# A fifth written order for stage one, with more of its loads held behind TensorE steps

## The chip, the cores and the metric

The kernel runs on one core of one Trainium2 chip. Its time is device microseconds of one execution, and a figure for a kernel is the median of several runs. The profile is one more execution, whose own time stands beside its span below.

## The reference

Three blocks follow one another; all is float32. The change is in the first.

```python
# block 1: per (batch 4, head 8), S = 576, D = 64
q_d, k_d, v_d = means over 4 neighbouring rows           # S/4 = 144 rows
out_up = repeat(softmax(scale * q_d @ k_d.T) @ v_d, 4)
mask = abs(i - j) < 4                                    # a local window
out = out_up + softmax(where(mask, scale * q @ k.T, -1e9)) @ v
# block 2: h = gelu(x @ w_in); u, v = halves; v normalised over features
x = x + (u * (w_sg @ v + b_sg)) @ w_out
# block 3: 4 experts of causal attention, top-2 gate by x @ w_gate
```

## The kernel before

The 4 x 8 heads go in 16 units u of two heads each (4 batches x 4 pairs); the functions below belong to `phase1`, the stage that takes about the first quarter of the span. One unit is these steps, named by a short name and the unit's number:

- Loads, all on SyncE's queue (SP): `lq`, `lk` (288 KB each), `lv` (288 KB, for the pooled branch), `lw` (320 KB, the windows of v). Their buffers come in rings, so that `lq`u and `lk`u also wait for unit u-3's transposes, `lv`u for `V`u-2, `lw`u for `Do`u-3.
- TensorE (PE): `Aq`, `Ak` transpose q and k; `Bm`, `Bs` write the mask and the windowed scores; `Bd` the pooled scores; `Cc`, `Ca` transpose the two softmax results; `Du`, `Do` multiply them with v.
- ScalarE (ACT): copies out of PSUM `aq`, `ak`, `cb`, `ca`, `du`, the exponentials `ey` and `ex`, small ones `yb`, `ne`.
- VectorE (DVE): `akd` (pooled k), maxima `ym`, `xm`, `xs` (subtract), sums `sx`, reciprocal `n`, and `dx`, which adds the two branches into `xT`.
- GpSimd (POOL): `aqd` (pooled q), `V` (pooled v), and the normalising multiplies `ny`, `nx`.

Woven in between is work for block 2: eight pieces of w_in are loaded (`fetch0` to `fetch7`, 512 KB each) and split into a high and a low part by `size` (ACT), `clamp`, `bits`, `stt1`, `stt2` (DVE), `hi` and `lo` (POOL). When all of batch 0 is in `xT`, `xhi` and `xlo` split it, and `mul0` to `mul3` (PE) are block 2's first products, with `gelu` behind each. `small` loads g_ln and b_sg. After stage one block 2 goes on with transposes of w_sg (`pwsg`, its loads `wsg` come next on SP) and the tiles `dv`, which read what `lo4` to `lo7` wrote.

Nothing of this is scheduled at run time. `ORDER` is a list of all 609 steps; the program is written out in that order, so each engine, and SP, does its own steps in the order in which the list has them, and a step that waits holds every later one of its engine. `GATE` names loads that additionally wait until a PE step has run: `lw0:Bm3` means that `lw0` is issued after `Bm3`. Behind a held load on SP every later load waits too.

PSUM has three `wide` tiles (two banks each: `Aq`, `Ak`, `Bm` with `Bs`, `Cc`, `Ca`, `Do`, `mul`) and two `narrow` ones (`Bd`, `Du`, `size`). `Steps.run` gives a step the tile that comes free first by its own table of costs, the first in its sequence where several are equal; a tile comes free when its readers are done.

Of the kernel before, what the change touches and what calls it, by code (L numbers as in the profile page):

```python
# [8 lines left out]
F32 = mybir.dt.float32  # L9
# [7 lines left out]
P = 128  # L17
# [3 lines left out]
def raw(ap):  # L21
# [1 line left out]


ORDER = """
    lk0 Ak0 lq0 lq1 lk1 Aq0 ak0 lq2 lk2 Aq1 aq0 Ak1 Bm0 aqd0 akd0 ak1 Bd0 aq1 Bs0 Aq2 aqd1 aq2 lq3 aqd2 Ak2
    akd1 ym0 xm0 Aq3 yb0 ak2 lq4 lk3 xs0 lv0 ey0 Bm1 Bd1 akd2 Bs1 ym1 xm1 aq3 V0 xs1 Ak3 ex0 ak3 sx0 Aq4 Bm2
    lk4 lk5 yb1 lq5 Bd2 ne0 aqd3 akd3 ey1 Bs2 n0 lv1 ny0 ex1 nx0 ym2 aq4 xm2 Ak4 xs2 ak4 sx1 aqd4 lk6 ex2 Bd3
    Bm3 akd4 Cc0 Ca0 lv2 sx2 ne1 yb2 Bs3 cb0 ym3 n1 nx1 fetch0 lq6 Ak5 ca0 ey2 Aq5 ak5 lq7 aq5 xm3 Ca1 yb3 xs3
    lw0 ny1 Cc1 Bm4 ne2 V1 ey3 Bd4 n2 akd5 ym4 ny2 Bs4 lk7 Du0 xm4 ca1 ex3 xs4 Ak6 cb1 du0 nx2 sx3 ak6 lv3 ex4  # L30
    Du1 yb4 du1 Cc2 lw1 aqd5 Do0 Bm5 fetch2 ne3 akd6 sx4 cb2 Bd5 dx0 ym5 fetch1 ey4 ne4 Bs5 size0 V2 Ca2 Aq6
    ca2 n3 yb5 aq6 ny3 lw2 V3 lw3 ey5 n4 xm5 Aq7 Ak7 clamp0 ak7 Du2 xs5 aq7 aqd6 bits0 nx3 stt10 Do1 stt20 Bm6
    Bd6 du2 dx1 Cc3 ex5 sx5 cb3 Ca3 ny4 ne5 ym6 hi0 ca3 Bs6 aqd7 lk8 yb6 Cc4 akd7 cb4 Do2 xm6 nx4 n5 Bd7 lq8
    xs6 lv4 Bm7 Ca4 nx5 ey6 dx2 ex6 ca4 ym7 Bs7 Du3 lk9 lo0 sx6 lv5 xm7 lq9 Aq8 ny5 ne6 lq10 Ak8 du3 V4 n6 yb7
    size1 xs7 Do3 clamp1 aq8 ey7 lw4 Ca5 nx6 Du4 lk10 ex7 ak8 ca5 V5 aqd8 du4 Cc5 fetch3 bits1 dx3 stt11 size2
    Ca6 akd8 lq11 Ak9 clamp2 bits2 cb5 stt21 Aq9 stt12 ak9 ny6 Do4 sx7 aq9 ca6 Bd8 aqd9 dx4 Bm8 Cc6 ym8 ne7 Bs8
    yb8 stt22 Ak10 Du5 cb6 xm8 ey8 n7 lv7 hi1 Aq10 ak10 xs8 akd9 Bm9 du5 lo1 akd10 size3 Bd9 clamp3 lv6 ny7
    aq10 Bs9 ym9 nx7 ex8 xm9 aqd10 yb9 lw5 fetch4 lk12 Aq11 Cc7 ey9 bits3 lk11 Bd10 lq12 lw6 xs9 Bm10 aq11
    stt13 V6 Do5 aqd11 ym10 lv8 Bs10 cb7 Ca7 yb10 ey10 stt23 ex9 Du6 dx5 sx8 V7 xm10 hi2 Ak12 du6 ca7 sx9 Du7
    lq13 ne8 Ak11 ak12 Aq12 size4 n8 xs10 ny8 ak11 lo2 aq12 clamp4 Bm11 akd12 nx8 Do6 V8 akd11 ne9 du7 aqd12  # L40
    Cc8 n9 Bd11 lk13 Bs11 dx6 lw7 ym11 bits4 fetch5 ex10 lq14 cb8 Ca8 stt14 xm11 yb11 sx10 Aq13 lk14 ey11 nx9
    lw8 Du8 xs11 ca8 aq13 ny9 Ak13 Do7 hi3 aqd13 ne10 stt24 ex11 dx7 n10 sx11 Bm12 Bd12 ak13 du8 Cc9 size5 Ca9
    ym12 ny10 nx10 lv9 akd13 Bs12 cb9 clamp5 Cc10 xm12 ca9 ne11 Ak14 n11 cb10 yb12 ak14 lo3 bits5 xs12 Aq14 Do8
    Bm13 hi4 ey12 lk15 lq15 ny11 V9 stt15 Bd13 aq14 ex12 dx8 Bs13 Ak15 aqd14 lv10 ym13 Aq15 stt25 nx11 ak15
    yb13 sx12 aq15 akd15 akd14 Du9 lw9 ne12 V10 Ca10 du9 xm13 Cc11 n12 xhi0 Bd14 ca10 xs13 nx12 lv11 xhi2 xlo2
    Do9 dx9 cb11 ym14 ey13 xhi1 Bm14 Ca11 ny12 Bs14 ca11 Du10 xm14 xs14 lw10 lv12 yb14 aqd15 Cc12 V11 hi5 Ca12
    du10 lw11 xhi3 fetch7 Bd15 V12 lo5 cb12 ey14 Bm15 xlo3 xlo1 Do10 xlo0 Bs15 Du11 ex13 lv13 ca12 sx13 ne13
    dx10 ym15 du11 lo4 ex14 size7 yb15 lw12 xm15 mul1 xs15 ey15 mul2 clamp7 ex15 fetch6 gelu1 sx14 Du12 bits7
    ne14 n13 gelu2 stt17 n14 V13 small ny13 du12 Do11 Do12 sx15 lw13 stt27 nx14 hi7 ne15 nx13 mul0 ny14 n15
    dx12 Cc13 dx11 size6 gelu0 Cc14 cb13 Ca14 clamp6 lo7 Ca13 Du13 ca14 cb14 lv14 ny15 ca13 lw15 lv15 lw14 Cc15  # L50
    bits6 nx15 stt16 mul3 cb15 V14 stt26 du13 Ca15 Do13 ca15 dx13 V15 Du14 gelu3 hi6 Du15 du15 lo6 Do14 Do15
    du14 dx14 dx15
""".split()
# [96 lines left out]
def tile_pooled_local_attention_gmlp_moe_attention(  # L150
# [50 lines left out]
    px = {}  # L201
# [52 lines left out]
    def phase1():  # L254
        with tc.tile_pool(name="s1", bufs=2, reuse_waits="tile") as p:
# [7 lines left out]
            pw = px["p"].tile([P, 2, 512], F32, name="wide", bufs=1)  # L263
# [260 lines left out]
            def d_x(u):  # L524
# [907 lines left out]
    with psum("ps1") as px["p"]:  # L1432
        phase1()
# [39 lines left out]
```

## Time and profile before

| what | us |
|---|---|
| median of 3 runs | 523.68 (521.07 to 525.8) |
| the profiled execution, its own time | 520.51 |
| span of that execution, first to last instruction | 518.5 |

The profiled execution has 2.0 us around its span, and lies 3.2 us under the median of the runs. Times below count from the start of the span. Stage one on PE goes from its first transpose at 5.63 us to the first `pwsg` transpose of block 2.

### The profile page before, as it was taken

The numbers are of one execution on the slowest core, as the hardware profiler recorded it, in microseconds if no ns is written. First come the engines' busy times: TensorE is split into PE (matmuls) and PEld (weight loads), VectorE is DVE, ScalarE is ACT, GpSimd is POOL, SyncE is SP. The second block draws the span as 40 slices with busy tenths as digits, with TensorE's granted clock in tenths as the row PEclk, the third lists the DMA queues.
The fourth block names the chain that finished last, engine by engine and source line by source line (L and its number), as shares of the span: only waits on it lengthen the run. The fifth ranks groups of instructions, "written<-read, shape, count | busy, mean of one in ns | idle before, by whom it ended". The sixth has DMA issues, their size and how long they took to land.

```text
span 518.5 us, 13684 instructions
## 1 busy us (share of the span) xinstructions
PE 504.5 (97%) x5405; PEld 460.9 (89%) x5405; DVE 350.3 (68%) x914; ACT 268.1 (52%) x676; POOL 252.9 (49%) x390
## 2 busy tenths in 40 slices
PE   9998898999999999999999999999999999999996
PEld 6986786889889899989998999999988989998885
DVE  4887898895869764542344137468699678868862
ACT  2886685785454450234013403356668558556761
POOL 4789689799253620360035106736447234333530
PEclk9999998999999999999999999999999999999999
DMA  8999599486500220000000001200000100011013
GB/s 204 224 226 191 153 212 210 109 202 164 163 1 2 82 61 1 1 0 1 1 1 0 1 1 31 73 2 2 2 0 1 43 21 22 21 42 43 20 62 102
DMA packets 43415, 35.02 MB, mean 68 GB/s; under 512 B 29976, under 2 KB 36376, under 8 KB 43352
## 3 DMA queue, kind: packets, MB, share of 16 engines
q1 hardware_dynamic: 43352, 34.15, 27.4%
q8 instruction: 43, 0.70, 0.6%
q14 instruction: 20, 0.16, 0.1%
HBM read 29.42 MB, written 4.72 MB: 66 GB/s over the span
## 4 chain that ended last, share of the span: by engine, by line
PE 83%; DVE 9%; issue 3%; ACT 2%; POOL 1%; DMA 1%; SPq 0%; ACTq 0%; DVEq 0%; POOLq 0%
PE wide L84 17%; PE f L84 10%; PE e L84 9%; PE du L84 7%; PE dv L84 6%; PE v L84 5%; PE i L84 5%; PE sc L84 5%; PE av L84 4%; PE gq L84 4%; PE gk L84 4%; PE tr L84 4%; PE narrow L84 3%; DVE xhla L606 1%; DVE wmn L694 1%
## 5 line engine op out<-in xcount | busy, mean ns | idle before, releaser
L249 POOL TENSOR_TENSOR gT<-z,gT 128x576 fp32r<-128x576 f32 x15 | 23.0, 1536 | 105.3 <-ACT gT L221 105.3
L1204 POOL TENSOR_SCALAR xT<-xT,sden,wt 128x128 f32<-128x128 f32 (+1 forms) x64 | 38.9, 609 | 57.8 <-DVE sden L1202 41.4
L84 PE MATMUL e<-wsgT,vn 128*128 128x288 f32 x384 | 56.6, 296 | 0.0
L84 PEld LDWEIGHTS e<-wsgT,vn 128*128 128x128 f32 x384 | 53.0, 188 | 0.3 <-DVE wsgT L735 0.2
L84 PE MATMUL f<-gT,wouts 128*128 128x288 f32 x384 | 52.1, 296 | 0.0
L84 PEld LDWEIGHTS f<-gT,wouts 128*128 128x128 f32 x384 | 51.4, 188 | 0.2 <-DVE wouts L701 0.2
L221 ACT CAST gT<-z 128x576 fp32r<-128x576 f32 x16 | 10.8, 675 | 78.1 <-DVE z L893 78.1
L1197 ACT ACTIVATE xT<-xT,smx 128x128 f32<-128x128 f32 (+4 forms) x72 | 42.3, 587 | 9.8 <-DVE smx L1190 7.6
L1190 DVE CUSTOM_DVE_ANT_0 xT<-sc,xT 128x128 f32<-128x128 f32 (+4 forms) x72 | 35.0, 487 | 18.2 <-PE sc L84 17.3
L84 PE MATMUL dv<-win,xhla 128*128 128x512 f32 x192 | 46.2, 395 | 0.5 <-ACT vg L803 0.5
L918 DVE TENSOR_TENSOR xT<-f,xT 128x576 f32<-128x576 f32 x16 | 12.1, 757 | 50.6 <-PE f L84 50.6
L84 PEld LDWEIGHTS dv<-win,xhla 128*128 128x128 f32 x192 | 35.5, 188 | 8.5 <-ACT vg L803 0.9
L84 PEld LDWEIGHTS du<-xhla,win 128*128 128x128 f32 x288 | 38.6, 188 | 0.2
L84 PE MATMUL du<-xhla,win 128*128 128x288 f32 x288 | 38.7, 295 | 0.0
L84 PE MATMUL tr<-ident,xT 128*128 128x128 f32 x192 | 33.0, 274 | 0.5 <-DVE smx L1190 0.5
L530 DVE TENSOR_TENSOR xT<-wide,up 64x288 f32<-64x288 f32 (+1 forms) x48 | 21.7, 451 | 12.6 <-PE wide L84 9.4
L84 PEld LDWEIGHTS tr<-ident,xT 128*128 128x128 f32 x192 | 23.7, 140 | 4.4 <-issue 0.9
L84 PE MATMUL i<-w,yT 128*128 128x512 f32 (+1 forms) x102 | 26.5, 395 | 0.0
L808 DVE BATCH_NORM_STATS2 bst<-vg 128x6 f32<-128x512 f32 x18 | 12.5, 692 | 17.4 <-ACT vg L803 17.3
L890 DVE SCALAR_TENSOR_TENSOR z<-e,gcol,bbc 128x576 f32<-128x576 f32 x16 | 13.0, 815 | 14.8 <-PE e L84 14.8
L84 PE MATMUL av<-aT,v 128*64 128x320 f32 (+3 forms) x192 | 22.7, 384 | 0.0
L84 PE MATMUL gq<-xhlb,w 128*128 128x288 f32 x144 | 21.8, 300 | 0.0
(215 smaller groups left out, 1335.2 us busy)
## 6 DMA issues: line engine op xcount, KB each, us to landing
vw<-in_v_dram SPq DMA_DIRECT2D x31, 160.0 KB
k<-in_k_dram SPq DMA_DIRECT2D x16, 288.0 KB
q<-in_q_dram SPq DMA_DIRECT2D x16, 288.0 KB
v<-in_v_dram SPq DMA_DIRECT2D x16, 256.0 KB
wst<-in_moe_w_in_dram SPq DMA_DIRECT2D x8, 512.0 KB
out_dram<-os SPq DMA_DIRECT2D x15, 256.0 KB
wst<-in_moe_w_out_dram SPq DMA_DIRECT2D x4, 512.0 KB
wsg<-in_moe_w_sg_dram SPq DMA_DIRECT2D x4, 288.0 KB
```

Source lines behind the costliest of these rows:

```text
L84: self.last = fn(*args, **kw)
L221: act.copy(o, i)
L249: e_lo.tensor_tensor(lo, src, raw(hi), op=ALU.subtract)
L530: dve.tensor_tensor(xT[dst, b, hp, a * HS : (a + 1) * HS].rearrange("c (s j) -> c s j", j=4), d["po"][src, a, :HS].rearrange("c (s j) -> c ...
L606: engines[e].tensor_tensor(xs[0][:, 1, kk], xT[:, 0, kk], raw(xs[0][:, 0, kk]), op=ALU.subtract)
L694: dve.scalar_tensor_tensor(d["mn"], d["t"][:, :, 1], -(2 ** 30), d["b"], op0=ALU.bitwise_and, op1=ALU.bitwise_or)
L808: dve.bn_stats(stt, g)
L890: dve.scalar_tensor_tensor(y2, o[:, :, :HS], gcol[:, dt : dt + 1], bbc.rearrange("p (a s) -> p a s", a=2), op0=ALU.mult, op1=ALU.add)
L918: dve.tensor_tensor(dst, os_[mt][:, :, :HS], dst, op=ALU.add)
L1190: dve.tensor_tensor_reduce(out=X[:, c0:c1], in0=os_[i][:, : c1 - c0], in1=tmask if i else cmask[:, z + c0 : z + c1] if r < NQ else cmask[: ...
L1197: act.activation(X, X, AF.Exp, bias=mx, scale=-1.0, accum_out=den)
L1204: pool.tensor_scalar(X, X, den, w, op0=ALU.mult, op1=ALU.mult)
```

## The change

The list `ORDER` is replaced by another one of the same 609 steps. `GATE` is replaced: by the count of its entries it names 35 loads before and 47 after; 22 loads are in both (only `lv13` with the same step), 13 are no longer held and 25 are newly held. The wide tile that the warm-up matmuls used (`pw`) comes first in the sequence of wide tiles where it came last. No instruction is added or removed, no shape and no engine changes.

The lists of loads on SP, with the step that holds one in brackets, are the shortest way to read the two versions. Before:

```
lk0 lq0 lq1 lk1 lq2 lk2 lq3 lq4 lk3 lv0(Bd0) lk4 lk5(Ak2) lq5 lv1 lk6 lv2 fetch0 lq6(Bd3) lq7(Bs3) lw0(Bm3) lk7 lv3 lw1 fetch2(Bs4) fetch1(Bd5) lw2 lw3(Aq6) lk8 lq8(Bd6) lv4(Bd6) lk9 lv5(Cc4) lq9 lq10 lw4(Ak8) lk10 fetch3 lq11(Ca6) lv7(Do4) lv6 lw5(Bs8) fetch4(Du5) lk12(Bd9) lk11(Aq10) lq12(Bd10) lw6 lv8 lq13(Du7) lk13 lw7 fetch5(Bd11) lq14 lk14 lw8(Ca8) lv9(Do7) lk15 lq15 lv10(Aq14) lw9(Do8) lv11(Du9) lw10 lv12(Bm14) lw11(Du10) fetch7(Bd14) lv13(Du11) lw12(Du11) fetch6(Bd15) small lw13(Du12) lv14(Do12) lw15 lv15 lw14(Ca14)
```

After:

```
lk0 lq0 lk1 lq1 lq2 lk2 lk3 lq3(Ak1) lv1(Ak1) lk4(Bm0) lk5 lq4(Bm1) fetch0(Bs1) lq6(Aq3) lq5(Ak3) lk6(Bd2) lv0 lw0(Ca0) lw1(Bm3) fetch1 lv2 lq8(Bs4) lq7(Ca1) lv3(Ak6) lk7(Do0) lw2 lq9 lw3(Bm6) lv4(Bm6) lk8(Do1) lk9(Ak7) lw4 lv5(Do2) fetch2(Bm7) lq10(Do3) lk10 lv6(Cc5) lq11 lk11(Du4) lw5 lw6(Ca5) fetch3 lv7(Aq10) lk12(Du6) lq12(Bs9) fetch4(Bd10) lv8(Bm10) lq13(Cc7) lk13(Ca7) lw7(Ak12) lq14(Bm11) fetch5 lk14(Ak13) lw8(Cc9) lv9 lk15(Cc9) lv10 lq15(Cc10) lw9 lv11 lw10(Cc11) lv12 lw11(Ca11) fetch6 lv13(Du11) lv14(Do11) fetch7(Bs15) lw12(mul3) lw13(Bs15) lw14(Bd15) lv15(Bs15) lw15 small(mul2)
```

The diff, with the order cut to its first and last lines:

```diff
 ORDER = """
-    lk0 Ak0 lq0 lq1 lk1 Aq0 ak0 lq2 lk2 Aq1 aq0 Ak1 Bm0 aqd0 akd0 ak1 Bd0 aq1 Bs0 Aq2 aqd1 aq2 lq3 aqd2 Ak2
-    akd1 ym0 xm0 Aq3 yb0 ak2 lq4 lk3 xs0 lv0 ey0 Bm1 Bd1 akd2 Bs1 ym1 xm1 aq3 V0 xs1 Ak3 ex0 ak3 sx0 Aq4 Bm2
...
-    dx12 Cc13 dx11 size6 gelu0 Cc14 cb13 Ca14 clamp6 lo7 Ca13 Du13 ca14 cb14 lv14 ny15 ca13 lw15 lv15 lw14 Cc15
-    bits6 nx15 stt16 mul3 cb15 V14 stt26 du13 Ca15 Do13 ca15 dx13 V15 Du14 gelu3 hi6 Du15 du15 lo6 Do14 Do15
-    du14 dx14 dx15
+    lk0 Ak0 lq0 lk1 Aq0 Ak1 aq0 ak0 akd0 lq1 aqd0 Aq1 Bm0 ak1 lq2 aq1 lk2 aqd1 lk3 Bd0 Bs0 Ak2 akd1 ym0 xm0 Aq2
+    yb0 lq3 xs0 ak2 ex0 Bm1 akd2 aq2 lv1 Bd1 lk4 lk5 Bs1 Ak3 sx0 Aq3 lq4 ey0 ne0 ym1 ak3 aqd2 V1 n0 nx0 aq3 yb1
+    Ak4 xm1 akd3 xs1 Bm2 Bd2 fetch0 lq6 ym2 ey1 lq5 ex1 aqd3 Bs2 xm2 sx1 ak4 yb2 Aq4 ny0 aq4 xs2 Bd3 ne1 Ca0
...
+    bits7 Cc13 stt17 Do12 nx15 mul2 dx12 cb13 lw15 Ca13 lo4 Ca14 gelu2 small ca13 Cc14 stt27 ny15 ca14 Ca15
+    stt16 stt26 Cc15 cb14 Du13 V15 Du14 Do13 du13 hi7 dx13 lo7 cb15 du14 ca15 Do14 hi6 Du15 du15 Do15 lo6 dx14
+    dx15
 """.split()
...
 GATE = dict(x.split(":") for x in """
-    lv0:Bd0 lw0:Bm3 lw3:Aq6 lv4:Bd6 lw4:Ak8 lk5:Ak2 lv5:Cc4 lw5:Bs8 lq6:Bd3 lq7:Bs3 lv7:Do4 lq8:Bd6 lw8:Ca8
-    lv9:Do7 lw9:Do8 lv10:Aq14 lq11:Ca6 lk11:Aq10 lv11:Du9 lw11:Du10 lq12:Bd10 lk12:Bd9 lv12:Bm14 lw12:Du11
-    lq13:Du7 lv13:Du11 lw13:Du12 lv14:Do12 lw14:Ca14 fetch1:Bd5 fetch2:Bs4 fetch4:Du5 fetch5:Bd11 fetch6:Bd15
-    fetch7:Bd14
+    lw0:Ca0 lv1:Ak1 lw1:Bm3 lq3:Ak1 lv3:Ak6 lw3:Bm6 lq4:Bm1 lk4:Bm0 lv4:Bm6 lq5:Ak3 lv5:Do2 lq6:Aq3 lk6:Bd2
+    lv6:Cc5 lw6:Ca5 lq7:Ca1 lk7:Do0 lv7:Aq10 lw7:Ak12 lq8:Bs4 lk8:Do1 lv8:Bm10 lw8:Cc9 lk9:Ak7 lq10:Do3
+    lw10:Cc11 lk11:Du4 lw11:Ca11 lq12:Bs9 lk12:Du6 lw12:mul3 lq13:Cc7 lk13:Ca7 lv13:Du11 lw13:Bs15 lq14:Bm11
+    lk14:Ak13 lv14:Do11 lw14:Bd15 lq15:Cc10 lk15:Cc9 lv15:Bs15 small:mul2 fetch0:Bs1 fetch2:Bm7 fetch4:Bd10
+    fetch7:Bs15
 """.split())
...
-                "wide": [px["p"].tile([P, 2, 512], F32, name=f"wide{i}", bufs=1) for i in range(2)] + [pw],
+                "wide": [pw] + [px["p"].tile([P, 2, 512], F32, name=f"wide{i}", bufs=1) for i in range(2)],
```

## Rows read from the trace of the kernel before

**Rows 1.** Windows: busy us (count) of PE, PEld, DVE, ACT, POOL; clock, DMA, GB/s.
```profile
80.00:90.00 10.00, 7.47 (x160) 6.19 (x153) 8.03 (x15) 4.97 (x14) 9.77 (x15) 0.89 1.13 211
...
110.00:120.00 10.00, 9.89 (x147) 9.29 (x146) 9.50 (x20) 7.45 (x19) 9.84 (x12) 1.00 0.73 182
```

**Rows 2.** Waits of PE, 0 to 134 us: total, times, longest.
```profile
PE wide L84 <- issue: 4.4, 5, 1.4
PE narrow L84 <- issue: 2.4, 1, 2.4
...
PE narrow L84 <- DVE kd L357: 0.3, 1, 0.3
PE wide L84 <- ACT bTs L221: 0.2, 1, 0.2
```

**Rows 3.** Timeline of PE, 0 to 70 us: start, duration, what, idle before.
```profile
35.16 0.46 PE L84 MATMUL wide<-kT,qT 64*64 64x64 f32 x17 [0.80 <-issue]
...
41.30 0.46 PE L84 MATMUL wide<-aTs,vw 64*64 64x57 f32 x16 [0.75 <-issue]
...
42.55 0.88 PE L84 MATMUL wide<-ident,Y 128*72 128x128 f32 x6
43.37 0.74 PE L84 MATMUL wide<-ident,X 128*128 128x128 f32 x5
...
47.80 0.33 PE L84 MATMUL wide<-aTs,vw 63*64 63x60 f32 x3 [1.42 <-issue]
...
51.91 1.16 PE L84 MATMUL wide<-ident,k 96*64 96x96 f32 x24
53.00 0.33 PE L84 MATMUL wide<-aTs,vw 64*64 64x60 f32 x5
54.62 0.79 PE L84 MATMUL wide<-aTs,vw 64*64 64x57 f32 x35 [1.30 <-issue]
```

**Rows 4.** Timeline of PE, 70 to 150 us.
```profile
80.64 0.45 PE L84 MATMUL wide<-kT,qT 64*64 64x64 f32 x13 [0.16 <-issue]
...
88.12 0.87 PE L84 MATMUL narrow<-kd,qd 64*64 64x144 f32 x5 [2.37 <-issue]
88.92 1.50 PE L84 MATMUL wide<-ident,Y 128*72 128x128 f32 x6
90.22 1.22 PE L84 MATMUL wide<-ident,X 128*128 128x128 f32 x5
...
109.64 7.01 PE L84 MATMUL wide<-xhla,win 128*128 128x288 f32 x48
...
132.71 0.77 PE L84 MATMUL pwsg<-ident,wsg 128*128 128x128 f32 x5
133.23 3.06 PE L84 MATMUL dv<-win,xhla 128*128 128x512 f32 x12
```

**Rows 5.** Windows cut at the ends of PE's stalls, columns as in Rows 1.
```profile
35.16:41.30 6.14, 5.39 (x126) 4.76 (x125) 4.64 (x9) 4.71 (x14) 5.37 (x8) 1.00 1.06 240
...
80.64:88.12 7.48, 5.11 (x126) 4.49 (x126) 6.46 (x12) 4.97 (x14) 7.25 (x13) 0.98 1.12 226
```

**Rows 6.** DMA queues, 47.8 to 51.9 us: packets, MB, share of 16 engines.
```profile
q1 hardware_dynamic: 540, 0.81, 102.4%
```

**Rows 7.** DMA queues, 51.9 to 54.6 us.
```profile
q8 instruction: 1, 0.02, 2.6%
```

**Rows 8.** DMA queues, 61.3 to 65.4 us, behind a boundary near 60.4.
```profile
q1 hardware_dynamic: 345, 0.59, 52.3%
q8 instruction: 1, 0.02, 1.4%
```

**Rows 9.** Timeline of POOL, its last step of stage one.
```profile
130.21 1.28 POOL L701 TENSOR_TENSOR win<-wmn,win 128x512 fp32r<-128x512 f32 x1
```

**Rows 10.** Timeline of DVE, the last three `xlo`.
```profile
107.20 3.03 DVE L606 TENSOR_TENSOR xhla<-xT,xhla 128x576 fp32r<-128x576 f32 x3
```

**Rows 11.** Timeline of SP's queue, loads of w_sg.
```profile
125.93 7.91 SPq L97 DMA_DIRECT2D wsg<-in_moe_w_sg_dram  x4
```

More of the change, by code (lines that the diff above doesn't have):

```diff
@@ L25 @@
 ORDER = """
-    lk0 Ak0 lq0 lq1 lk1 Aq0 ak0 lq2 lk2 Aq1 aq0 Ak1 Bm0 aqd0 akd0 ak1 Bd0 aq1 Bs0 Aq2 aqd1 aq2 lq3 aqd2 Ak2
-    akd1 ym0 xm0 Aq3 yb0 ak2 lq4 lk3 xs0 lv0 ey0 Bm1 Bd1 akd2 Bs1 ym1 xm1 aq3 V0 xs1 Ak3 ex0 ak3 sx0 Aq4 Bm2
-    lk4 lk5 yb1 lq5 Bd2 ne0 aqd3 akd3 ey1 Bs2 n0 lv1 ny0 ex1 nx0 ym2 aq4 xm2 Ak4 xs2 ak4 sx1 aqd4 lk6 ex2 Bd3
-    Bm3 akd4 Cc0 Ca0 lv2 sx2 ne1 yb2 Bs3 cb0 ym3 n1 nx1 fetch0 lq6 Ak5 ca0 ey2 Aq5 ak5 lq7 aq5 xm3 Ca1 yb3 xs3
-    lw0 ny1 Cc1 Bm4 ne2 V1 ey3 Bd4 n2 akd5 ym4 ny2 Bs4 lk7 Du0 xm4 ca1 ex3 xs4 Ak6 cb1 du0 nx2 sx3 ak6 lv3 ex4
@@ L31 @@
[L31 to L49, printed above, removed]
-    dx12 Cc13 dx11 size6 gelu0 Cc14 cb13 Ca14 clamp6 lo7 Ca13 Du13 ca14 cb14 lv14 ny15 ca13 lw15 lv15 lw14 Cc15
@@ L51 @@
-    bits6 nx15 stt16 mul3 cb15 V14 stt26 du13 Ca15 Do13 ca15 dx13 V15 Du14 gelu3 hi6 Du15 du15 lo6 Do14 Do15
-    du14 dx14 dx15
+    lk0 Ak0 lq0 lk1 Aq0 Ak1 aq0 ak0 akd0 lq1 aqd0 Aq1 Bm0 ak1 lq2 aq1 lk2 aqd1 lk3 Bd0 Bs0 Ak2 akd1 ym0 xm0 Aq2
+    yb0 lq3 xs0 ak2 ex0 Bm1 akd2 aq2 lv1 Bd1 lk4 lk5 Bs1 Ak3 sx0 Aq3 lq4 ey0 ne0 ym1 ak3 aqd2 V1 n0 nx0 aq3 yb1
+    Ak4 xm1 akd3 xs1 Bm2 Bd2 fetch0 lq6 ym2 ey1 lq5 ex1 aqd3 Bs2 xm2 sx1 ak4 yb2 Aq4 ny0 aq4 xs2 Bd3 ne1 Ca0
+    akd4 ey2 Cc0 Bm3 ex2 aqd4 Bd4 cb0 lk6 n1 lv0 Bs3 ym3 sx2 ca0 nx1 xm3 ny1 Aq5 ne2 V0 xs3 yb3 n2 lw0 Ak5 Bm4
@@ new lines @@
+    ey3 aq5 Cc1 ak5 lw1 nx2 akd5 Ca1 ym4 ex3 sx3 cb1 Bs4 yb4 ey4 ny2 Du0 du0 Aq6 size0 xm4 ne3 fetch1 Du1 xs4
+    Ak6 ca1 aq6 lv2 clamp0 Cc2 bits0 n3 stt10 ak6 Ca2 aqd5 lq8 stt20 lq7 Do0 akd6 cb2 dx0 aqd6 ex4 ny3 Bm5 Bd5
+    du1 ym5 Bs5 ca2 xm5 xs5 Cc3 yb5 sx4 Aq7 lv3 Bd6 Bm6 V2 nx3 cb3 aq7 ex5 ym6 lk7 Do1 ey5 Bs6 Ca3 V3 dx1 lw2
+    lq9 ne4 sx5 Du2 Do2 lw3 ca3 lv4 hi0 xm6 Ak7 du2 aqd7 n4 Du3 xs6 nx4 yb6 ey6 ak7 ne5 ny4 lk8 Aq8 dx2 Ca4 lk9
+    n5 Cc4 size1 du3 akd7 ex6 ca4 Bd7 nx5 aq8 lw4 Do3 sx6 lv5 clamp1 V4 ym7 Bm7 cb4 Bs7 ne6 n6 dx3 nx6 Aq9 yb7
@@ new lines @@
+    aq9 lo0 xm7 Ak9 xs7 fetch2 ny5 ny6 ey7 lq10 ak9 bits1 Ak8 ex7 Cc5 aqd8 stt11 Du4 stt21 ak8 Do4 akd8 Bm8
+    aqd9 du4 akd9 dx4 Bd8 ym8 lk10 size2 lv6 hi1 Bs8 cb5 lq11 Ca5 yb8 ca5 ey8 sx7 Aq10 ne7 aq10 clamp2 Ak10 V5
+    lk11 Du5 V6 xm8 lw5 bits2 ak10 Ca6 Cc6 du5 xs8 lw6 n7 ex8 ca6 ny7 akd10 sx8 cb6 fetch3 Bm9 Bd9 stt12 stt22
+    nx7 lv7 Bs9 ym9 Aq11 Du6 aqd10 xm9 Do5 yb9 ne8 n8 lk12 aq11 du6 Do6 xs9 ny8 Bd10 ey9 ex9 nx8 aqd11 dx5 Ak11
+    dx6 size3 Ca7 lq12 ak11 Cc7 V7 Bm10 fetch4 ca7 lv8 clamp3 cb7 sx9 lq13 ym10 bits3 Bs10 xm10 akd11 Ak12 lo1
@@ new lines @@
+    ne9 yb10 ey10 hi2 ak12 Aq12 xs10 ex10 lk13 Du7 Cc8 stt13 stt23 lw7 n9 lo2 sx10 du7 Ca8 hi3 cb8 aq12 Bd11
+    size4 akd12 ca8 ne10 Bm11 V8 ym11 clamp4 bits4 Bs11 xm11 Aq13 yb11 Ak13 ey11 Du8 lq14 ny9 aq13 stt14 aqd12
+    Do7 fetch5 nx9 xs11 Cc9 du8 Bd12 stt24 ak13 cb9 ex11 Bm12 lk14 Ca9 lo3 lw8 n10 dx7 Bs12 lv9 size5 ca9 Aq14
+    ym12 sx11 ny10 Ak14 xm12 nx10 akd13 aq14 clamp5 ne11 yb12 xs12 Cc10 lk15 lv10 ak14 n11 Do8 aqd13 bits5
+    aqd14 stt15 cb10 Bm13 lq15 stt25 Ca10 Bs13 ex12 ca10 sx12 Bd13 ey12 nx11 dx8 lw9 ym13 akd14 V9 ne12 Ak15
@@ new lines @@
+    Du9 ny11 ak15 xm13 Cc11 n12 xs13 du9 akd15 lv11 Aq15 Bd14 yb13 ey13 V10 nx12 Bm14 cb11 Do9 ym14 aq15 Bs14
+    xhi0 Ca11 lw10 ny12 lv12 V11 xhi1 aqd15 ex13 V12 yb14 ca11 xhi2 dx9 Du10 Cc12 du10 ey14 Ca12 cb12 hi4 Du11
+    hi5 xhi3 xm14 xs14 xlo0 Do10 lw11 ex14 Bm15 Bd15 Bs15 fetch6 xlo1 xlo2 du11 Du12 xlo3 dx10 sx13 lv13 ym15
+    sx14 ca12 ne14 yb15 lo5 xm15 V13 Do11 n14 xs15 ne13 lv14 fetch7 ey15 mul3 mul1 ex15 n13 lw12 lw13 du12 sx15
+    nx14 ny13 dx11 lw14 V14 ne15 gelu1 size7 gelu3 lv15 size6 nx13 clamp7 n15 ny14 clamp6 mul0 gelu0 bits6
```

## The prediction

> **What bounds the kernel now.** Three views, in this order. First the windows of ten microseconds over stage one: PE is busy for nearly all of each, but in the worst it has 7.47 us of 10, and DVE and POOL run at 9.5 us of 10 or more in the late one [rows 1]. So no engine is free enough to hide much, and PE is the one that sets the end. Second, PE's waits from 0 to 134 us, to see what its idle time is for: 4.4 + 2.4 = 6.8 us are put down to "issue", that is to nothing the profile shows, and only 0.3 + 0.2 us to another engine [rows 2]. The order before, then, hardly ever makes PE wait for a step. Third, the timeline of PE, to see where the 6.8 us lie: six stalls, 0.80, 0.75, 1.42, 1.30, 0.16 and 2.37 us, sum 6.80 [rows 3, 4]. Every one of them falls inside a step (ahead of the last 3 products of one `Do`, of the last 5 of one `Bd`), where no step's dependence can be. And they come at a fixed count: between the ends of two stalls PE has run 126 matmuls and 125 or 126 weight loads [rows 5]. That is a block of PE's program, and PE stands until the next block has been fetched.
>
> The DMA queues show when. From 47.8 us, where a stall ends and a new block begins, to 51.9 us the data queue keeps the engines busy at 102% and no packet of the instruction queue starts [rows 6]; the one packet of it comes between 51.9 and 54.6 us [rows 7], and PE goes on at 54.62 [rows 3]. Behind a boundary near 60.4 us, with data at 52% of the engines, a packet came as well and no stall followed [rows 8]. I read this as: a block that is asked for while loads crowd the engines comes several us late, and PE's next block of 5 to 7 us is too short to cover it.
>
> **What the change can win at all.** Stage one on PE lasts from 5.63 us (front) to 132.71 [rows 4], 127.1 us. Without the six stalls (6.8), the two waits (0.5) and the slow clock it would be 118.7. The clock: behind the 2.37 us stall the granted clock is 0.89 in that window [rows 1], which is the lower level, 1.2 GHz, for a part of it; six transposes then last 1.50 us and five 1.22, against 0.88 and 0.74 [rows 3, 4], 0.62 + 0.48 = 1.1 us. So 127.1 - 118.7 = 8.4 us, 1.6%, is the most that any order of the same steps can give.
>
> **The loads.** To see how each list crowds the DMA engines I walk down it: PE's steps are added up (a transpose step of q or k is 53.00 - 51.91 = 1.09 us, `Cc` 43.37 - 42.55 = 0.82 [rows 3], the rest in the same way), a load is issued when its gate or its ring lets it go and the loads ahead of it on SP are out, and the queue drains at the 211 KB per us of the crowded window [rows 1]. This gives no time for the kernel, only a count. Past the first 10 us, the list before issues 31 loads with over 1000 KB queued and 11 with over 1200 KB; these 11 lie in five places, the largest with 1610 KB (`lq14 lk14 lw8`, just ahead of the 0.16 and 2.37 us stalls; `fetch2`, `fetch1`, `lw2`, `lw3` precede the first two). The list after issues 14 with over 1000 KB, and four with over 1200, in two places: `fetch1 lv2` (1312 KB) early, and `fetch3 lv7` (1412 KB) in the middle. The reason is plain in the lists: `fetch2` no longer comes beside `fetch1` and two window loads but waits for `Bm7`, and of `lk14 lw8 lk15 lq15` three are newly held.
>
> Two places in which a stall is likely, and one of the places near 1100 KB, make three stalls where there were six. At the mean of the six, 6.8 / 6 = 1.13 us, three are 3.4 us: **-3.4 us**. The bounds are 0 (as many stalls as before, or worse ones) and -6.8. The slow clock came with the one long stall; with shorter ones it goes: **-1.1 us**, between 0 and -1.1.
>
> The Trainium skill, page "Runtime: NRT & Kernel Launch", section "Instruction fetch mechanics", says that a sequencer fetches the next 16 KiB block, 256 instructions, by its own DMA queue while it runs the current one, and that the crossing is "mostly hidden". The block of 126 + 126 instructions agrees [rows 5]; "mostly hidden" does not, at 6.8 us here [rows 2]. By that word there would be nothing to win, and the sum would be the costs below alone.
>
> **The order on the engines.** All 609 steps stay, so no engine's work changes; what can change is who waits for whom. Between `Bs` and `Ca` of a unit lie on average 17.2 us of PE's steps after and 16.7 before, between `Aq` and `Bd` 7.1 and 6.5, between `Ca` and `Do` 8.2 and 9.7, between `Cc` and `Du` 5.3 and 6.5: longer ahead of the softmax, shorter behind it, none plainly worse. Two places I price.
>
> (1) The start, where the steps are chained most tightly: `Bm2` needs `xs1`. After, DVE has `sx0`, `n0` and `akd3` ahead of it, which before came behind; some 1.5 us, of which the earlier `Bd1` and `Bs1` (one transpose step, 1.09 us) take back most. **+0.4 us**, between 0 and 1.5. `aq0` is put ahead of `ak0` on ACT, but `Bd0` waits for POOL's `aqd0` as before: nothing, hidden by that.
>
> (2) The end. POOL's last step `lo6` ends at 130.21 + 1.28 = 131.49 [rows 9], and the `dv` products that read it begin at 133.23 [rows 4]: 1.7 us to spare. From `Bs13` on, PE's steps left are 35.4 us in both lists, POOL's 33.5 before and 35.9 after. If POOL keeps the pace of the lists, the spare 1.7 becomes -0.7: **+0.7 us**, between 0 (the first `dv` products need other blocks of w_in, and POOL had idle time that the stalls caused) and 2.4.
>
> Edits with nothing: the first product with w_in waits for the last `xlo` (the first product starts at 109.64, the last `xlo` ends at 107.20 + 3.03 = 110.23 [rows 4, 10]); up to it DVE has 92.8 us of steps in both lists, and its next, `dx10` with 1.4, must now free the tile of `mul3`; PE's side has become 1.2 us longer, so this cancels. `small` waits for `mul2` and the w_sg loads queue behind it on SP; they were issued 132.71 - 125.93 = 6.8 us ahead of their use [rows 4, 11] and now will be about 5.8: nothing, 0 to 1 if that is too short. The turned sequence of wide tiles changes which tile each step writes; at the end `pw`, the first tile that block 2 takes over, was last read by `gelu3` and now by `dx13`, with three more PE steps ahead of its reuse to cover that: nothing, at most 1.4 (a `dx`).
>
> **Sum** against the profiled execution: 520.51 - 3.4 - 1.1 + 0.4 + 0.7 = 517.1; that execution lies 3.2 us under the median of the runs, so in terms of that median **520.3**. The bounds of the terms run from -7.9 to +6.3 us, 515.8 to 530.0; both ends at once are unlikely.
>
> **The rivals.** A measurement of this kernel tells 1%, about 5 us, from no change.
>
> A, the forecast, stalls halved: 518 to 522. Chance 0.47.
>
> B, late blocks do not depend on how the loads are held. For it: how late a block comes does not follow the traffic closely. At a DMA share of 1.06 PE lost 0.75 us, at 1.12 it lost 2.37 [rows 3 to 5]. Then the six stalls stay, 6.8 us in other places, the clock too, and the costs add 1.1: 523.7 + 1.1 = 524.8. The Trainium skill, page "DMA: Bandwidth & Descriptors", section "Queues, rings and completion order", is on this side: each engine turns from queue to queue after every packet, so a fetch on its own queue would wait for one data packet, not for the queued megabyte. The four us without a packet at 102% [rows 6] speak against it. Chance 0.22.
>
> C, stalls all but gone: one of 1 us is left and the rest of the order costs nothing: 523.7 - 5.8 - 1.1 = 516.8, and with POOL's idle time gone as well down to 515.3. For it: 14 crowded issues where there were 31. Against: two of the places are as crowded as before. Chance 0.19.
>
> D, slower: held loads arrive late. SP goes in order, and by the same walk `lk4`, `lq4`, `lq5`, `lq7`, `lk14`, `lq15` and `lw7` are drained only 2.6 to 3.2 us ahead of the PE step that reads them. If landing and the mistakes of the walk take more than that, each of the seven stops PE; at 1.5 us each, 10.5 us against 4.5 won and 1.1 lost: 523.7 + 7.1 = 530.8. Against: the list before had eight loads drained 1.8 to 3.0 us ahead by the same count, and PE never waited for one [rows 2]. Chance 0.12.
>
> **How the numbers follow.** The likeliest is A, 520.3. For 8 in 10 I leave out the lower third of C and most of D: 515.5 to 527. Faster by over 1% (under 518.4): C with 0.19 and the lower edge of A with 0.1, 0.29. Slower by over 1% (over 528.9): most of D and a tail of B, 0.11. Within 1%: 0.60.
>
> **What would show it.** In the profile after: PE's "issue" waits to about 134 us near 3.4 us instead of 6.8 (A), near 6.8 (B), under 1.5 (C); still inside steps, 126 matmuls apart; the first `pwsg` near 129.3 us; the clock at full speed in every window. The start is right if the mask of unit 2 begins about 18.7 us, the end if `dv` waits less than a microsecond for POOL. D would show as waits of PE, ACT or POOL for loads. I am wrong if the stalls stay while the loads are spread, or if waits for other engines, 0.5 us now, pass 3 us.

## The result, and the profile after

The changed kernel took 516.5 us (median of 18 executions, 513.81 to 520.11) beside 521.36 for the kernel before (18, 517.58 to 525.8): a ratio of 0.9906, interval 0.9881 to 0.9930. In a second comparison, with e6 to e8 below, it took 516.86 beside 520.52, 0.9951, interval 0.9920 to 0.9982. So some 4 us are gained, a little under 1%. The forecast was 520.3 in a range of 515.5 to 527. Ratios leave out executions more than 1.5% above the fastest of their kernel, medians don't; for e1 to e4 that leaves out 10 of the 24 executions of the kernel before, so that there a ratio lies up to 0.4% above the quotient of the two medians.

Two executions of the changed kernel were profiled, and they differ. The first took 519.69 us (span 517.8), near the upper end of its 18; the second (run e5 below) took 516.89 (span 514.9), at the median of its 12. The kernel before has its profile at 520.51, inside the spread of its medians in four comparisons (520.38 to 521.55).

PE's waits up to 134 us in the first profile after, against [rows 2] (total, times, longest):

```profile
PE wide L85 <- issue: 2.0, 3, 1.2
PE narrow L85 <- issue: 1.9, 1, 1.9
PE narrow L85 <- POOL vd L385: 1.8, 1, 1.8
...
PE wide L85 <- DMA q<-in_q_dram: 0.9, 1, 0.9
PE wide L85 <- DMA k<-in_k_dram: 0.8, 1, 0.8
PE wide L85 <- DVE X L421: 0.5, 1, 0.5
PE wide L85 <- DMA vw<-in_v_dram: 0.3, 1, 0.3
PE wide L85 <- POOL Y L465: 0.2, 1, 0.2
```

The same view of the second profile:

```profile
PE narrow L85 <- POOL vd L385: 2.0, 1, 2.0
...
PE wide L85 <- POOL Y L465: 1.0, 2, 0.8
PE wide L85 <- ACT bTs L222: 0.7, 2, 0.4
PE wide L85 <- ACT kT L222: 0.6, 1, 0.6
PE wide L85 <- DMA q<-in_q_dram: 0.5, 1, 0.5
PE wide L85 <- DVE X L421: 0.5, 1, 0.5
PE wide L85 <- ACT Y L441: 0.3, 1, 0.3
```

What to see: the stalls for nothing shown fell from 6.8 us to 3.9 in one execution and to none in the other. In their place PE waits for other engines and for loads: 4.5 us (2.5 for engines, 2.0 for loads) and 5.6 us (5.1 and 0.5), where it was 0.5. (A wait of 1.3 us ahead of the warm-up matmuls, the same in all profiles, is left out of these sums and of those below.) The largest of PE's new waits, about 2 us, is one place in the written order. The timeline of PE in the first profile has it and the end of the stage, beside [rows 3, 4]:

```profile
57.56 0.38 PE L85 MATMUL wide<-aTs,vw 64*64 64x57 f32 x10 [1.17 <-issue]
...
64.76 0.41 PE L85 MATMUL narrow<-bTs,vd 128*64 128x144 f32 x2 [1.92 <-issue]
...
109.02 0.71 PE L85 MATMUL narrow<-bTs,vd 128*64 128x144 f32 x8 [1.81 <-POOL vd L385]
...
110.40 9.83 PE L85 MATMUL wide<-xhla,win 128*128 128x288 f32 x72
...
131.77 0.77 PE L85 MATMUL pwsg<-ident,wsg 128*128 128x128 f32 x5
132.29 1.89 PE L85 MATMUL dv<-win,xhla 128*128 128x512 f32 x7
```

The 8 `bTs,vd` products at 109.02 are `Du12`. It waits for `V12`, and `Do11` and `mul3` (110.40) stand behind it. POOL and DVE around it:

```profile
105.33 1.24 POOL L383 TENSOR_TENSOR vd<-v 72x256 f32<-72x256 f32 x1
...
107.84 1.12 POOL L385 TENSOR_TENSOR vd<-vd,vda 72x256 f32<-72x256 f32 x1
...
111.46 0.74 POOL L383 TENSOR_TENSOR vd<-v 72x256 f32<-72x256 f32 x1
...
128.31 1.27 POOL L702 TENSOR_TENSOR win<-wmn,win 128x512 fp32r<-128x512 f32 x1
```
```profile
104.26 4.12 DVE L607 TENSOR_TENSOR xhla<-xT,xhla 128x576 fp32r<-128x576 f32 x4
```

`V12`'s three operations last 1.12 to 1.24 us beside the four `xlo` of DVE, and 0.74 without them (111.46). In the kernel before, `Du12` stood behind two `mul` steps, so PE had 7 us of other work there [rows 4].

In the second profile the stage ends at 129.08, where it ended at 132.71 before [rows 4] and at 131.77 in the first. That is nearly the whole difference of the two executions (2.7 us of 2.8):

```profile
129.08 0.76 PE L85 MATMUL pwsg<-ident,wsg 128*128 128x128 f32 x5
```

The stalls that are left come again where a block of 126 matmuls ends. A window of the first profile from one stall's end to the next, columns as in [rows 1, 5]:

```profile
57.56:64.76 7.20, 5.28 (x126) 4.65 (x126) 6.21 (x11) 4.08 (x13) 5.46 (x9) 1.00 1.22 197
```

The DMA engines are full in it, as in the blocks that came late before. The granted clock is 1.00 in every window of ten microseconds of stage one in both profiles, so the slower level of [rows 1] is gone.

### The profile page after: what moved, and what is told of

It reads as the page before. It is cut to its first block, busy times and chain, and to the rows that moved or that the text cites. A ratio compares the mean times of both kernels' runs of the same rounds, so it can differ in the third digit from the quotient of the medians.

```text
span 517.8 us, 13684 instructions
## 1 busy us (share of the span) xinstructions
PE 502.8 (97%) x5405; PEld 460.0 (89%) x5405; DVE 351.4 (68%) x914; ACT 268.4 (52%) x676; POOL 252.5 (49%) x390
## 4 chain that ended last, share of the span: by engine, by line
PE 71%; DVE 9%; POOL 9%; DMA 4%; issue 4%; ACT 2%; SPq 0%; DVEq 0%; POOLq 0%
PE wide L85 10%; PE f L85 10%; PE e L85 9%; PE v L85 5%; PE du L85 5%; PE i L85 5%; PE sc L85 5%; PE dv L85 5%; PE av L85 4%; PE gq L85 4%; PE gk L85 4%; PE tr L85 4%; DMA q<-in_q_dram 2%; DMA k<-in_k_dram 1%; PE narrow L85 1%
## 5 line engine op out<-in xcount | busy, mean ns | idle before, releaser
L809 DVE BATCH_NORM_STATS2 bst<-vg 128x6 f32<-128x512 f32 x18 | 12.5, 693 | 17.6 <-ACT vg L804 17.6
```

The source lines that it names most:

```text
L809: dve.bn_stats(stt, g)
```

## The experiments

Theory: loads that crowd the DMA engines make PE's next program block late, and the new list of loads takes most of that away; what the order of the steps costs comes back as waits. Rivals: the blocks are late whatever the loads do (rival B of the prediction); the gain is the order of the steps, or the tiles' sequence, and not the loads.

### e1: the loads of after on the steps of before

Order of the computing steps and every step's tile as before; all loads in after's sequence (but for `lv0` and `lv1`, which change places), each held to the step of the old order at which PE has done as much work.

```diff
 GATE = dict(x.split(":") for x in """
-    lv0:Bd0 lw0:Bm3 lw3:Aq6 lv4:Bd6 lw4:Ak8 lk5:Ak2 lv5:Cc4 lw5:Bs8 lq6:Bd3 lq7:Bs3 lv7:Do4 lq8:Bd6 lw8:Ca8
...
+    lk3:Ak0 lq3:Aq1 lv0:Aq1 lk4:Bm0 lk5:Aq2 lq4:Ak2 fetch0:Bd1 lq6:Ak3 lq5:Ak3 lk6:Bd2 lv1:Bd2 lw0:Bm3
...
```

> Order of the engines' steps and PSUM tiles as before; all 64 loads after the first six are let go at the same sum of PE's steps as after (by the walk 14 of them with over 1000 KB queued, 31 before). Theory, the loads' timing sets the time: PE's issue waits to 134 us fall from 6.8 to some 3 to 4.5 us and the ratio to before is 0.990 to 0.995. Rival, the new order of the engines' steps sets it: the ratio is 0.998 to 1.003, with issue waits of 5 to 8 us.

Measured: 531.38 us, 1.0221 of before (1.0160 to 1.0282); its profile took 528.33. PE's waits:

```profile
PE wide L93 <- DVE kd L366: 2.2, 1, 2.2
...
PE wide L93 <- DMA q<-in_q_dram: 1.8, 3, 0.7
PE wide L93 <- DMA k<-in_k_dram: 1.4, 1, 1.4
...
PE narrow L93 <- issue: 1.1, 1, 1.1
```
```profile
121.85 0.71 PE L93 MATMUL narrow<-bTs,vd 128*64 128x144 f32 x8 [1.07 <-issue]
```

"Issue" is down from 6.8 to 1.1 us with no step of PE moved, and even the 1.1 us isn't a late block: it lies ahead of a whole step, `Du12`, which takes the tile that ACT reads until 121.75 us (`ey15`). But with the rest of the view (issue included) PE waits 11.9 us, mostly for loads and for other engines, and these waits also give late blocks time to come, so the run alone doesn't show that the stalls follow the loads. The ratio is neither the theory's (0.990 to 0.995) nor the rival's (0.998 to 1.003): the kernel is slower than either parent. The slower level of the clock has a part in that (0.85, 0.83 and 0.83 in three windows of ten microseconds). On the old order these loads cost more than they save.

### e2: the loads of before on the steps of after

The mirror of e1 (`lv2` and `lv7` keep after's place); after's order, tiles and their sequence.

```diff
 GATE = dict(x.split(":") for x in """
-    lw0:Ca0 lv1:Ak1 lw1:Bm3 lq3:Ak1 lv3:Ak6 lw3:Bm6 lq4:Bm1 lk4:Bm0 lv4:Bm6 lq5:Ak3 lv5:Do2 lq6:Aq3 lk6:Bd2
...
+    lq3:Aq0 lq4:Ak1 lk3:Ak1 lv1:Bd0 lk4:Bs0 lk5:Bm1 lq5:Bm1 lv0:Bd1 lk6:Aq3 fetch0:Bm2 lq6:Bd3 lq7:Bd4
...
```

> Order of the engines' steps and PSUM tiles as after; the loads are let go at the same sum of PE's steps as before, but for lv2 and lv7, which the new order can only take later (by the walk 21 loads with over 1000 KB queued). Theory, the loads' timing sets the time: issue waits of 5 to 7 us and a ratio to before of 0.997 to 1.003. Rival, the order of the steps: ratio 0.988 to 0.993, as after.

Measured: 531.69, 1.0240 (1.0183 to 1.0298); its profile took 530.74.

```profile
PE wide L92 <- DMA vw<-in_v_dram: 6.4, 3, 5.8
PE wide L92 <- issue: 3.6, 3, 1.4
```

One window load comes 5.8 us late. Neither expected ratio came (0.997 to 1.003, or 0.988 to 0.993). The steps of after with these loads are no gain; 3.6 us of stalls, fewer than the 5 to 7 that the theory wanted, lie between the two kernels and tell neither way.

### e3 and e6: the changed kernel with the old sequence of tiles

```diff
-                "wide": [pw] + [px["p"].tile([P, 2, 512], F32, name=f"wide{i}", bufs=1) for i in range(2)],
+                "wide": [px["p"].tile([P, 2, 512], F32, name=f"wide{i}", bufs=1) for i in range(2)] + [pw],
```

> The changed kernel with the warm-up's tile last in the sequence of wide tiles, as before. Theory, the turn only renames tiles: ratio to before 0.988 to 0.993, as the changed kernel. Rival, the turn is worth something at the hand-over to block 2 or at the start: ratio 0.995 or more, with a wait of PE at the first transpose of q and k or at the first of w_sg.

Measured: 519.28, 1.0018 (0.9981 to 1.0055) of before. The edit was run again beside the changed kernel:

> The changed kernel with the wide tiles in their sequence of before, again, so that it stands beside the changed kernel on the same chip. Theory: the first pwsg product waits for the eviction dx15 of the last wide tile (2.45 us in the first profile of this edit, none in the changed kernel), and nothing else differs, so 2.4 us slower than the changed kernel, a ratio to it of 1.0046. Rival one: the sequence also sets which tile each step of stage one waits for, and the edit costs 5 to 6 us, the distance of the two ratios measured so far (0.9906 and 1.0018). Rival two, as the prediction put it: at most a dx, 1.4 us.

Measured: 520.54, 1.0002 (0.9969 to 1.0035); the changed kernel beside it 516.86 (e5, below). Timelines of PE and DVE in e3:

```profile
127.24 0.81 PE L85 MATMUL wide<-aTs,vw 64*64 64x60 f32 x40
130.50 0.74 PE L85 MATMUL pwsg<-ident,wsg 128*128 128x128 f32 x5 [2.45 <-issue]
```
```profile
126.15 4.25 DVE L531 TENSOR_TENSOR xT<-wide,up 128x288 f32<-128x288 f32 x9 [4.38 <-PE wide L85]
```

The stage's last matmul (`Do15`) ends at 128.05, but the first `pwsg` starts at 130.50, when the nine evictions `dx13` to `dx15` have ended at 130.40. The profile calls it "issue"; by the times the releaser is the last `dx`. `Steps.run` goes by a tile's place in the sequence, so which steps of stage one share a tile is the same with and without the turn; what differs is which of the three is `pw`. By that rule `pw` is now last written by `Do15`, with the turned sequence by `Do13`. e6 has the same wait (2.45 us). So the rival of e3 was right, and the theory that the turn only renames tiles was wrong at the hand-over: the turn is worth 2.45 us on this order. The 3.7 us between the medians of e6 and e5 contain that; what the rest is, stays open. Without the turn the change as a whole is worth nothing that can be measured.

### e7: the turn alone, on the kernel before

The same line of code, turned in the kernel before.

> The kernel before, with its order and its held loads, and of the change only the wide tiles' new sequence. By the written order and the rule of the slots the tile whose banks stage two takes first is then last written by Do15 and emptied by dx15, where in the kernel before it was last written by mul3. If the hand-over to stage two is what the sequence is worth, this edit costs here what it saves in the changed kernel: 2 to 2.5 us more than before, a ratio of 1.004 to 1.005, with a first pwsg product that waits 2 us or more. If the new sequence is a gain by itself, whatever the order, the ratio is below 0.998.

Measured: 524.11, 1.0055 (1.0019 to 1.0090). The first `pwsg`, which had no wait [rows 4], has one:

```profile
135.48 1.30 PE L84 MATMUL pwsg<-ident,wsg 128*128 128x128 f32 x5 [2.48 <-issue]
```

The time is 3.6 us longer, 2.5 of them in this wait. So the sequence has no value of its own; it has to hand `pw` over early on the order at hand. The old sequence did that on the old order, the new one does it on the new. The profile also has the old order's stalls again, 6.5 us (5.1 + 1.4) in five places, so they belong to that list and not to one execution.

### e4: few window loads

The kernel before without `lw3` to `lw15`: units 3 and on multiply windows of v that were not loaded for them, and that part of the output is left out.

```diff
                 b, hp = units[u]
                 vw = st.setdefault(u, {})["vw"] = vws[u % 3]
+                if u >= 3:
+                    return
```

> The kernel before without the window loads lw3 to lw15 (26 transfers of 160 KB or less in 256-byte packets); the products read the windows of units 0 to 2 again, so that part of the output is left out. Every other step stands. Theory, PE's program blocks come late because of the loads' traffic: issue waits to 134 us fall from 6.8 to under 2 us, the ratio to before is 0.983 to 0.990. Rival, the blocks come late whatever the loads do: issue waits of 5 to 8 us, ratio 0.997 to 1.003.

Measured: 520.23, 1.0018 (0.9975 to 1.0061); its profile took 522.33. Waits of PE, and windows in the part where the loads are missing:

```profile
PE wide L84 <- issue: 4.8, 5, 1.4
PE wide L84 <- DVE xT L532: 2.1, 1, 2.1
PE narrow L84 <- issue: 1.5, 1, 1.5
```
```profile
60.00:70.00 10.00, 9.65 (x248) 8.55 (x248) 9.88 (x17) 7.11 (x19) 6.01 (x9) 1.00 0.44 130
...
100.00:110.00 10.00, 7.66 (x180) 6.72 (x178) 9.78 (x12) 7.11 (x22) 9.77 (x13) 0.86 0.38 113
```

By the marks set before the run this is the rival's outcome: stalls of 5 to 8 us and a ratio of 0.997 to 1.003, where the theory wanted under 2 us. Where the stalls lie is another matter, and was read only afterwards. Past 60 us, with the engines at 32 to 65%, no stall is left, where the kernel before has two of 2.5 us in all; up to 57 us, with a DMA share of up to 1.09, there are 6.3 us where it had 4.3 [rows 3, 4]. The first three of them (at 14.49, 21.14 and 27.32 us, 2.9 us in all) come before the first load that is missing, under the same loads with which the kernel before has none there: the stalls of one execution are also a matter of chance. What was won late was lost again, to these and to the wait for `xT` of DVE, with the clock at 0.86 behind it. So e4 doesn't settle the question; e9 and e10 do.

### e5 and e8: the changed kernel again, and with `Du12` behind `mul3`

> The changed kernel once more, unaltered, beside the next three on one chip, for a second profile of it and a ratio in the same company. If its 4.9 us are a property of the order and not of the company it was first timed in, 0.988 to 0.994 of the kernel before. In its second profile the theory of bunched loads wants 2 to 5 us of PE stalls that wait for nothing shown (6.8 before, 3.9 in its first profile), and the wait of Du12 for V12 at 109 us, 1.8 us in its first profile, should stand again at 1.5 to 2.1 us, since it comes of the written order.

Measured: 516.86 us, 0.9951 (0.9920 to 0.9982). Its profile stands above: no stalls at all, below the expected 2 to 5 us; the wait of `Du12` is there, 2.0 us. The ratio lies just outside the expected 0.988 to 0.994, which its interval overlaps.

```diff
-    hi5 xhi3 xm14 xs14 xlo0 Do10 lw11 ex14 Bm15 Bd15 Bs15 fetch6 xlo1 xlo2 du11 Du12 xlo3 dx10 sx13 lv13 ym15
-    sx14 ca12 ne14 yb15 lo5 xm15 V13 Do11 n14 xs15 ne13 lv14 fetch7 ey15 mul3 mul1 ex15 n13 lw12 lw13 du12 sx15
...
+    ex14 Bm15 Bd15 Bs15 fetch6 xlo1 xlo2 du11 xlo3 dx10 sx13 lv13 ym15 sx14 ca12 ne14 yb15 lo5 xm15 V13 Do11
+    n14 xs15 ne13 lv14 fetch7 ey15 mul3 Du12 mul1 ex15 n13 lw12 lw13 du12 sx15 nx14 ny13 dx11 lw14 V14 ne15
...
```

> The changed kernel with the TensorE step Du12 moved behind mul3. In the changed kernel PE waits 1.8 to 2.0 us for V12 of POOL before Du12, with Do11 and mul3 queued behind it, although the xlo splits that mul3 needs are done 2 us before it starts. Theory: the waits that took the place of the stalls are on the path, so this wait goes, mul3 starts 1.5 to 2 us earlier, and the time falls by 1 to 2 us, 0.996 to 0.998 of the changed kernel. Rival: POOL's queue ends the stage (V13 to V15, hi and lo stay where they are), the 2 us come back as a wait at Du13 to Du15 or dv, and the time stays within 0.2% of the changed kernel.

Measured: 516.37 us, 0.9921 (0.9884 to 0.9958) of before, 0.999 of e5's median: the lowest of all kernels, but not to be told from the changed one by time. The timeline of PE in its profile (515.83):

```profile
105.95 3.45 PE L85 MATMUL wide<-xhla,win 128*128 128x288 f32 x24 [0.89 <-DVE xT L531]
...
128.16 0.76 PE L85 MATMUL pwsg<-ident,wsg 128*128 128x128 f32 x5
```

The wait for `V12` is gone, and `mul3` now waits 0.89 us for the tile that `dx10` empties. The stage ends at 128.16, 0.92 us ahead of e5, though 1.7 us of stalls fell on this execution and none on e5. That speaks for the wait having been on the path, in one execution of each. The medians don't show it: they differ by 0.5 us, not by the 1 to 2 that were expected, and within 0.2% is the rival's mark, though the wait that the rival wanted at `Du13` to `Du15` or `dv` isn't there. What an average execution gains stays open at this spread.

### e9 and e10: no load held

Both kernels with an empty list of holds; each load is issued as soon as its ring and the loads ahead of it let it.

```diff
 GATE = dict(x.split(":") for x in """
-    lw0:Ca0 lv1:Ak1 lw1:Bm3 lq3:Ak1 lv3:Ak6 lw3:Bm6 lq4:Bm1 lk4:Bm0 lv4:Bm6 lq5:Ak3 lv5:Do2 lq6:Aq3 lk6:Bd2
...
 """.split())
```

> The changed kernel with its order and tiles, but none of the 47 loads held: SP issues each as soon as its ring and the loads ahead of it let it. No load comes later than in the changed kernel; by the walk of the prediction 51 loads are issued with over 1000 KB queued and 47 with over 1200, where the changed kernel has 14 and 4. Theory of bunched loads: the issue stalls come to 7 us or more (3.9 and 0 us in two profiles of the changed kernel), waits for loads stay under 1 us, and the time is 3 to 8 us above the changed kernel, 0.998 to 1.010 of the kernel before. Rival, late blocks independent of how the loads are held: stalls as in the changed kernel, 0 to 4 us, and a time of 0.990 to 0.996 of the kernel before.

> The kernel before with none of its 35 loads held, its order and tiles as they were. By the walk 53 loads are issued with over 1000 KB queued and 48 with over 1200, where the kernel before has 31 and 11. Theory of bunched loads: issue stalls well above the 6.8 us of the kernel before, 9 us or more, and a time 2 to 5 us above it, a ratio of 1.004 to 1.010. Rival, late blocks independent of how the loads are held: 6 to 7 us of stalls and a ratio within 0.3% of 1.

Measured: e9 528.86, 1.0131 (1.0068 to 1.0194); e10 533.33, 1.0181 (1.0058 to 1.0305). Waits of PE and two windows in e9:

```profile
PE narrow L81 <- issue: 6.4, 4, 2.9
PE wide L81 <- issue: 2.5, 1, 2.5
PE narrow L81 <- POOL vd L381: 1.9, 1, 1.9
```
```profile
40.00:50.00 10.00, 8.11 (x185) 7.09 (x185) 5.07 (x9) 3.96 (x12) 5.98 (x9) 0.83 0.77 143
...
80.00:90.00 10.00, 9.12 (x141) 8.29 (x141) 5.39 (x9) 3.82 (x9) 6.32 (x10) 0.66 1.20 199
```

and waits in e10:

```profile
PE wide L81 <- issue: 6.7, 6, 2.3
PE narrow L81 <- issue: 3.1, 2, 2.6
```

With the same steps and tiles, 8.9 us of stalls instead of 3.9 and 0, and 9.8 instead of 6.8 (6.5 in e7): the stalls do depend on how the loads are held, and rival B is out. Both are slower than was expected of them, and in e9 the slower level of the clock makes up the difference (e10 has windows at 0.66, 0.83 and 0.83): e9's two windows behind the stalls of 2.92 and 2.50 us have a granted clock of 0.83 and 0.66, two later ones 0.93 and 0.90. (The later two stand behind the 1.9 us wait for `V12`; behind the 2.0 us of the same wait in e5 the clock stayed at 1.00, so what makes it fall isn't shown.) A window of 10 us at 0.83 loses up to 1.7 us of work; the four lose up to 6.8. Stalls of 8.9, less 3.2 us of waits for others that they covered (2.4 in place of e5's 5.6), and 6.8 make 12.5; the stage ends 12.8 us later than in e5 (141.84 against 129.08).

## Why the prediction came out right, step by step

**The bound** held: the gain is in PE's idle time in stage one. From the first `pwsg` to the end, 387.8 us are left in both kernels (520.51 - 132.71 and 516.89 - 129.08).

**The loads** (-3.4): right in kind, as e9 and e10 show, and sized too small. The changed kernel's two profiles have 3.9 and 0 us of stalls, and its close relatives e3, e6 and e8, with the same loads, 2.0, 1.7 and 1.7; the mean of the five is 1.9, so the term was nearer -4.9. The walk ranked the lists well (with over 1000 KB queued 53, 51, 31, 21 and 14 issues; stalls 9.8, 8.9, 6.8, 3.6 in e2 and 1.9), but it does not tell where one falls: the block that cost 1.92 us in one execution cost nothing in the other. The Trainium skill, page "Runtime: NRT & Kernel Launch", section "Instruction fetch mechanics", calls the crossing of a block boundary mostly hidden; that is so in e5, without a stall, and with 8.9 us in e9 it is not.

**The clock** (-1.1): right in kind; 1.00 in every window of both profiles. It was sized a little too small: the five products at 88.12 us took 0.87 us at the slower level [rows 4] and were not counted; the same five took 0.53 us in e7, also right behind a stall. That makes -1.4.

**The order on the engines** (+1.1 in all) is the step that was mis-sized. It priced the start and POOL's end. Neither cost anything: the mask of unit 2 began at 18.12 and 19.07 us (18.52 before; the forecast says 18.7, though its own +0.4 makes that 18.9), and in the second profile PE was 0.8 us later than in the first from its second step on; POOL's last `lo6` (128.31) ended at 129.58 in the first profile, 2.7 us ahead of `dv`. But "none plainly worse" was wrong. The waits for other engines and loads rose from 0.5 to 4.5 and 5.6 us, so the term was +4 to +5 in these two executions; in e3 and e6, with the same list, the waits were 2.5 and 3.4, +2 to +3. For engines alone they were 2.5 and 5.1 us: in the second profile past the 3 us that the prediction had named as the mark of its failing. The largest part could have been read from the two lists: `Du12`, behind two `mul` steps before, stands ahead of `mul3` after, with `V12` behind `aqd15` on POOL. The prediction looked at `xlo` and `dx10` there and called it even. Two held loads came late too, one of rival D's seven and one newly held, `lq5` (0.92 us) and `lk9` (0.78), as a part of the sum and not as the 10 us of that rival.

**The sum** came out because the two errors have opposite signs, which is luck. They may not be independent: while PE waits for a step, its next block has time to come. Against the second profile: -6.8 of stalls, +5.1 of waits, -1.4 of clock, -3.1 together, where the stage ended 3.6 us earlier (0.5 us is not assigned). Against the first: -2.9, +4.0 and -1.4, -0.3 together, where it ended 0.9 us earlier. The forecast had -3.4 and 129.3 us for the first `pwsg`; measured were 129.08 and 131.77. On the base of the profiled execution it said 517.1; 516.5 and 516.9 were measured. The 3.2 us that were added because that execution lay under the median of three were an error of the base: over 7 to 35 executions before has 520.4 to 521.6. Of the rivals' numbers 516.5 is that of C (516.8), not that of A (518 to 522); but C wanted an order that costs nothing, and that isn't what the runs show.

**The turned sequence** (nothing): right as a difference of the two kernels, for the reason given (`pw` is left early in both). What the prediction did not see is what it stands for, beyond its "at most 1.4": 2.45 us if the list is changed without it (e3, e6), and as much if it is changed without the list (e7).

## What to carry to other kernels

A list of loads, an order of steps and the tiles' sequence that were fitted together are one thing: the two hybrids of loads and steps were over 2% slower than both versions, and a list with the other's sequence of tiles lost 2.5 us at the hand-over. When a stall goes, list what each step on the bounding engine waits for next in the new order, step by step, ahead of the sum: here that gave back 2 to 5 of the 6.8 us. Take the base from many executions when the change is as small as their spread.

## What the hardware showed that was not expected

That PE's stalls are late program blocks is seen in the packets. In the ten profiles that have stalls inside steps there are 47 up to 134 us, and each ends 1.2 to 1.8 us after a 16 KB packet of the instruction queue has moved (in the first profile after, the packet that starts at 61.59 us takes 1.41, and PE goes on at 64.76).

The same program block can come late in one execution and in time in the next. It begins at 57.56 us in the first profile after and at 56.15 in the second, and the stall behind it was 1.92 us in the first and none in the second. The DMA queues in the first two microseconds of it (packets, MB, share of 16 engines), first profile and second:

```profile
q1 hardware_dynamic: 303, 0.44, 110.1%
```
```profile
q1 hardware_dynamic: 232, 0.38, 82.3%
q8 instruction: 1, 0.02, 4.3%
```

That fits the traffic. The next block of the second profile, 61.42 to 63.6 us, doesn't: its packet came as soon with the data queue far busier.

```profile
q1 hardware_dynamic: 1388, 0.36, 134.8%
q8 instruction: 1, 0.02, 3.9%
```

So crowding makes stalls more frequent (e9, e10), but what decides for one block stays open.

A GpSimd operation of 72x256 takes 0.74 us as a rule and 1.12 to 1.24 us while DVE runs the `xlo` subtractions (above), 1.4 us more for the three of `V12`. The kernel before shows the same within one `V12`: the first of its operations begins beside the last `xlo`, which ends at 110.23 [rows 10], the next behind it.

```profile
109.60 1.22 POOL L382 TENSOR_TENSOR vd<-v 72x256 f32<-72x256 f32 x1
110.78 0.73 POOL L383 TENSOR_TENSOR vda<-v 72x256 f32<-72x256 f32 x1
```

The Trainium skill, page "SBUF — State Buffer", section "Who interferes with whom", says that a DVE operation with two SBUF inputs contends with a GpSimd operation that reads SBUF, since its second input comes through an interface that the two share. `xlo` has two such inputs, and the slowing from 0.74 to 1.24 us agrees with that.
